# Linear attention and two MLPs on one core: the numerator in plain float32 on half arrays, and five k buffers

## The chip, the cores and the metric

The kernel runs on one core of a Trainium2 chip. The metric is the device time of one execution in microseconds, as the median of several runs. For the kernel before it is 980.39 us (3 runs, 980.27 to 983.37). Engines are named as in the profile: PE (TensorE; PEld are its weight loads), DVE (VectorE), ACT (ScalarE), POOL (GpSimd), SP (SyncE, which issues all transfers here).

## The reference

```python
def phi(x):                                   # 128 random features of each head
    h = einsum('bhsd,md->bhsm', x, omega) - sum(x * x) / 2
    return exp(h - max(h)) / sqrt(m)
q_p, k_p = phi(q * scale), phi(k * scale)     # 4 batches, 8 heads, 576 tokens, width 64
kv  = einsum('bhsm,bhsd->bhmd', k_p, v)
num = einsum('bhsm,bhmd->bhsd', q_p, kv)
den = einsum('bhsm,bhm->bhs', q_p, sum(k_p, axis=2)) + 1e-6
x = (num / den) as 2304 tokens x 512
x = mish(x @ w_in)  @ w_out                   # 512 -> 2048 -> 512
x = silu(x @ w2_in) @ w2_out                  # 512 -> 2048 -> 512
```

## The kernel before

The attention runs unit by unit. There are 36 k units (four batches of nine, each 128 tokens of four heads; the middle unit of a batch has 64 tokens for either group of heads). Each loads a buffer `kin`, projects it (`kproj`: two plain float32 products into `kpj`), takes the maximum and the bias on DVE, exponentiates on ACT into `kf`, and accumulates `kv` and the column sums (`kacc`, into `acc`). `k_finish` then copies the sum of a batch into `kv`, in a high part (`kvh`, ACT) and a low part (`kvl`, DVE), and spreads the denominators (`zb`, `zt`, `zz`). There are 36 q units: nine blocks of 256 tokens, two groups of four heads, two halves of 128 tokens. Each loads `qin`, projects (`qproj`: either plain float32, or split into high and low parts and three fast products), takes maximum, exponent and denominator, scales the features (`fn`), and transposes them on PE (`tr`, into `tp`); ACT copies the transposed features out (`hiT`). After the second half of a group the numerator (`num`, into `xp`) multiplies them with `kv`, and the result goes to a tile `X` in high and low parts (`xev`, `xlo`). Four steps of the first MLP (`H` and `Y`, products into `h` and `y`) follow for every block, with weights that were converted and split beforehand (`conv`, from `wr` to `wt` to `W`). When the attention is done, the rest of both MLPs runs in blocks of 512 columns.

The numerator exists in two forms. For the first two blocks (`NUM4 = 2`) it is four plain float32 products of 256 columns with a stationary operand of 128 columns (`num4`, tiles `FTf` and `kvf`): 64 columns of one head beside 64 columns of zeros, and the two heads of a pair add up into one 128-row result. For the other seven blocks it is split (`num`): high and low parts of the features (`hiT`, `loT`) and of `kv`, three fast products (`mm3`, the helper at lines 273 to 275, also used by the MLPs) for each head and pair, 12 in all, or 24 where a block crosses the border of two batches. Three of the nine blocks do. All features stand in one buffer `FT`, or one `FTf`.

The order of all instructions is written by a planner (`Plan`). Every task has an engine, a cost and a key (a due time; `KSPAN` is the span of a batch of k units in it, the table `OFF` adds to it, and `VAR` says which engine does a task). The planner simulates the engines, picks buffers from rings, and emits the tasks in the simulated order; on the chip each engine then runs its own list in order and waits for semaphores. `SHARED` is what it charges a DVE task that runs beside POOL. Where it foresees a gap on PE early on, it emits small filling products into a tile that is about to be written (line 420), which keep PE active and compute nothing. Transfers are all issued by SP in one list; one whose buffer is not free yet holds up those behind it. The `kin` ring has three buffers, and for the first seven units (`KIN0`) also the two `X` tiles.

Of the kernel before, what the change touches and what calls it, by code (L numbers as in the profile page):

```python
# [9 lines left out]
F32 = mybir.dt.float32  # L10
F32R = mybir.dt.float32r
# [8 lines left out]
P = 128  # L20
# [15 lines left out]
KSPAN = 7.6  # L36
EPS = 0.1

NUM4 = 2
# [4 lines left out]
VAR = dict(sqk="DPPDDDDDDDDDDAPDDDDDDDPPDDDDDDPDPPPP",  # L44
           sqq="DPDDPPDDDPDDDPPDDPDPDPPDADDPDPPDDDAA",
           den="DDDDDDDDDPDDPDDDDDDDPPDPPPDPDDDDDPDD",
           fn="PPPPPPPDPDPPDPPAPPPPDPPPDPPPDPPPDPPP",
           gl="PDDPDPDPDPDPDDDDPPPPPDDDDDDDDDDDPDDD",
           qlo="PDDDDPPPDPDDPDDDPPPPPDPDDPPDPDDPPDDP",
           wl="DDPDPDDPDPPPDDPP",  # L50
           wsg="DDDDDDDDDDDDDDDDDDDDDDDDDDDDDDDDDDDDDDDDDDDDDDDDD",
           xlo="DDDDDPDDDDDDDDPPPP",
           spl="S4444SSSSSSSSSSSSSSS4SSS44SSSSSSSSSS")
HORIZON = 21.0
OFF = {'H': -0.73, 'K*': -3.2, 'K0': -0.01, 'K1': 0.11, 'K10': -0.4, 'K17': -0.19, 'K28': -0.47, 'K4': 0.02, 'K7': -0.74,
# [11 lines left out]
       22.43, 'xll': -31.58, 'xlo': -8.73, 'xst': -1.34, 'xsth': -13.01, 'xstl': 8.31, 'xt': -2.1, 'zb': -3.35, 'zt': -1.62,  # L67
       'zz': 0.64}
# [4 lines left out]
SHARED = dict(wb0=0.8, wo0=0.6, ws0=0.5, wl0=0.5, wb1=0.8, wo1=0.6, ws1=0.5, gl=0.6, ksqr=2.5, qsqr=2.5, den=1.3, fn=0.6,  # L73
              qlo=0.5, xtbx=1.2, sa=1.5, kba=5.0, kbb=5.0, qba=5.0, qbb=5.0, dea=5.0)


def kind_of(name):
# [6 lines left out]
    if (k[0] == "q" and k not in ("qp", "qd")) or k in ("fz", "den", "dea", "der", "fn", "tr", "hiT", "loT", "num", "xev", "xlo", "xf", "xst"):  # L84
        return k, "Q*", "Q" + re.findall(r"\d+", name)[0]
# [178 lines left out]
def performer_two_mlps(ctx: ExitStack, tc: tile.TileContext, qin, kin, omT, w1, w2, out):  # L264
# [136 lines left out]
    D = 2.0  # L401
# [26 lines left out]
    T("FTf", "-", 0, -99, lambda: None, new=[("FTf", "FTf")], writes=["FTf"])  # L428
    T("FT", "-", 0, -99, lambda: None, new=[("FT", "FT")], writes=["FT"])
# [50 lines left out]
    def k_unit(b, j):  # L480
# [3 lines left out]
        if j == 0:  # L484
            def zero():
                POOL.memset(t[f"kv{b}"][:, :, :, 64:128].bitcast(F32), 0.0)

            T(f"kvo{b}", "Pool", 0.5, key, zero, writes=[f"kv{b}:{x}{g}" for x in "hl" for g in range(2)],
              new=[(f"kv{b}", "kv"), (f"z{b}", "z")])
            if not b:  # L490
                T("kvof", "Pool", 0.3, key, lambda: POOL.memset(t["kvf"][:, :, 64:128], 0.0), writes=["kvf:0", "kvf:1"], new=[("kvf", "kvf")])
# [36 lines left out]
    def k_finish(b, g, key):  # L528
# [8 lines left out]
        def kvh():  # L537
            src, dh, dl = parts()
            ACT.copy(dh, src)

        def kvl():
            src, dh, dl = parts()
            DVE.tensor_tensor(dl, src, dh.bitcast(F32), ALU.subtract)
# [593 lines left out]
```

## Time and profile before

| | kernel before |
|---|---|
| median of the runs | 980.39 us |
| the profiled execution, its own time | 987.46 us |
| its span, first to last instruction | 985.7 us |
| PE busy | 957.7 us (97%) |
| PEld / DVE / ACT / POOL busy | 890.0 / 631.5 / 519.2 / 327.8 us |
| granted clock, mean | 0.987 of full |
| moved by DMA | 102.56 MB, mean 104 GB/s |

Busy times of PE are to be read with care: the end of a product is modelled and lies behind the start of the next one, and filling products count as busy. What a product costs in a stream is the distance from its start to that of the next. Plain float32 products stand as two records each. The share of the whole span hides the stages: in the first 140 us the k units, the q units, the conversion of the weights and the loads are all under way together; after that PE is nearly without a gap.

### The profile page before, as it was taken

What the parts mean: (1) busy time and instruction counts of PE and PEld (TensorE: products, weight loads), DVE (VectorE), ACT (ScalarE), POOL (GpSimd) and SP (SyncE); (2) the same over time, 40 slices, a digit from 0 to 9 for tenths busy, and PEclk for the clock granted to TensorE, in tenths of its full rate; (3) what the DMA queues carried; (4) which work ended last, traced back from release to release, by engine and by line L of the source; (5) the groups of instructions that cost most, each with busy time, mean ns of one, the idle gap of its engine ahead of it and who ended that gap; (6) DMA issues with size and microseconds to landing.
All of it is one profiled execution on the core that took longest, in us unless ns stands there. A gap on an engine that the chain in (4) does not pass through costs nothing.

```text
span 985.7 us, 18121 instructions
## 1 busy us (share of the span) xinstructions
PE 957.7 (97%) x6671; PEld 890.0 (90%) x6671; DVE 631.5 (64%) x1686; ACT 519.2 (53%) x1128; POOL 327.8 (33%) x308
## 2 busy tenths in 40 slices
PE   7888999999999999999999989999999999999998
PEld 6777899999999999989899988898998898898898
DVE  6989876877776566744665789538446774353422
ACT  5676777787677655443444454445444543433221
POOL 2223213424553165430622374406223433213010
PEclk8999899999999999999999999999999999999999
DMA  7665335333231124205144244122332201311202
GB/s 248 209 221 186 103 110 165 97 109 110 94 118 55 44 87 126 99 22 192 44 150 150 87 134 131 57 86 65 108 108 86 86 22 44 125 58 54 86 1 86
DMA packets 50360, 102.56 MB, mean 104 GB/s; under 512 B 4960, under 2 KB 17504, under 8 KB 50272
## 3 DMA queue, kind: packets, MB, share of 16 engines
q1 hardware_dynamic: 50272, 101.41, 31.6%
q8 instruction: 52, 0.85, 0.4%
q14 instruction: 36, 0.29, 0.1%
HBM read 78.85 MB, written 22.54 MB: 103 GB/s over the span
## 4 chain that ended last, share of the span: by engine, by line
PE 78%; DVE 11%; DMA 4%; issue 3%; ACT 3%; POOL 1%; SPq 0%; POOLq 0%; DVEq 0%; ACTq 0%
PE y L275 12%; PE y L274 12%; PE y L273 12%; PE ha L273 5%; PE ha L274 4%; PE ha L275 4%; PE h L273 3%; PE h L274 3%; PE h L275 3%; PE hb L273 3%; PE hb L274 3%; PE hb L275 3%; DMA kin<-in_kin_dram 2%; PE acc L516 2%; PE kpj L505 2%
## 5 line engine op out<-in xcount | busy, mean ns | idle before, releaser
L843 DVE TENSOR_TENSOR gl<-e,gh 128x512 fp32r<-128x512 f32 x132 | 109.6, 837 | 142.3 <-ACT gh L841 140.3
L841 ACT CAST gh<-e 128x512 fp32r<-128x512 f32 x144 | 89.1, 623 | 177.8 <-PE y L274 171.3
L273 PE MATMUL y<-gh,W 128*128 128x256 f32 (+1 forms) x548 | 179.0, 327 | 0.0
L275 PE MATMUL y<-gl,W 128*128 128x256 f32 (+1 forms) x548 | 178.0, 325 | 0.0
L274 PE MATMUL y<-gh,W 128*128 128x256 f32 (+1 forms) x548 | 178.0, 325 | 0.0
L275 PEld LDWEIGHTS y<-gl,W 128*128 128x128 f32 x548 | 103.3, 189 | 9.6 <-DVE gl L843 0.2
L273 PEld LDWEIGHTS y<-gh,W 128*128 128x128 f32 x548 | 103.4, 189 | 8.3
L274 PEld LDWEIGHTS y<-gh,W 128*128 128x128 f32 x548 | 103.4, 189 | 8.2
L273 PE MATMUL h<-X,W 128*128 128x256 f32 x288 | 83.6, 290 | 0.0
L274 PE MATMUL h<-X,W 128*128 128x256 f32 x288 | 81.6, 283 | 0.0
L275 PE MATMUL h<-X,W 128*128 128x256 f32 x288 | 81.5, 283 | 0.0
L763 POOL TENSOR_TENSOR LHL<-Lqf,LX 128x512 fp32r<-128x512 f32 x19 | 25.4, 1343 | 161.4 <-ACT LX L762 161.1
L895 DVE TENSOR_TENSOR Lfz<-Lfz,ha 128x256 f32<-128x256 f32 x48 | 20.2, 420 | 84.2 <-PE ha L275 60.7
L736 ACT ACTIVATE wa<-wr 128x512 f32<-128x512 f32 x64 | 43.4, 681 | 51.9 <-DVE wt L747 29.6
L840 ACT ACTIVATE e<-hb 128x512 f32<-128x512 f32 x48 | 28.7, 598 | 51.8 <-DVE hb L895 51.8
L747 DVE SCALAR_TENSOR_TENSOR wt<-wa,wt 128x512 int32<-128x512 int32 x64 | 54.8, 861 | 0.9
L274 PEld LDWEIGHTS h<-X,W 128*128 128x128 f32 x288 | 55.0, 191 | 0.1
L273 PEld LDWEIGHTS h<-X,W 128*128 128x128 f32 x288 | 54.9, 191 | 0.1
L275 PEld LDWEIGHTS h<-X,W 128*128 128x128 f32 x288 | 54.9, 191 | 0.0
L505 PE MATMUL kpj<-cst,kin 128*128 128x256 f32 x144 | 41.4, 414 | 9.2 <-DMA kin<-in_kin_dram 8.0
L516 PEld LDWEIGHTS acc<-kin,kf 128*128 128x128 f32 (+1 forms) x320 | 42.1, 204 | 7.3 <-ACT kf L476 5.3
L648 POOL TENSOR_TENSOR qf<-qf,smq 128x512 f32<-128x512 f32 x28 | 31.2, 1117 | 50.9 <-DVE smq L639 13.9
(546 smaller groups left out, 3024.5 us busy)
## 6 DMA issues: line engine op xcount, KB each, us to landing
wr<-in_w_dram SPq DMA_DIRECT2D x64, 512.0 KB, 3.9
kin<-in_kin_dram SPq DMA_DIRECT2D x35, 386.0 KB, 3.9
qin<-in_qin_dram SPq DMA_DIRECT2D x36, 256.0 KB, 3.3
xf<-sx SPq DMA_DIRECT2D x18, 256.0 KB, 2.5
yp<-stg SPq DMA_DIRECT2D x18, 256.0 KB, 2.1
stg<-yp SPq DMA_DIRECT2D x18, 256.0 KB, 5.2
y<-stg SPq DMA_DIRECT2D x18, 256.0 KB, 2.4
Lqf<-y SPq DMA_DIRECT2D x17, 256.0 KB, 3.0
```

The costliest lines, as they stand in the source:

```text
L273: PE.matmul(o, s_hi, m_hi, start=first, stop=False, skip_group_check=True)
L274: PE.matmul(o, s_lo, m_hi, start=False, stop=False, skip_group_check=True)
L275: PE.matmul(o, s_hi, m_lo, start=False, stop=last, skip_group_check=True)
L505: PE.matmul(t[pj][:, jj * 256:(jj + 1) * 256], t[res][:, jj * P:(jj + 1) * P], t["cst"][:, P:P + 256], start=True, stop=True, skip_group_c ...
L516: PE.matmul(a[:, h, :], t[f][r0:r1, h * NF:(h + 1) * NF], v[r0:r1, h, :], start=first and h == 0, stop=last, skip_group_check=True)
L648: (DVE if fn_e == "DVE" else POOL).tensor_tensor(x, x, smq[:, r, 5, :, None].to_broadcast([P, 4, NF]), ALU.mult)
L736: T("wm" + c, "ACT", 0.57, key, lambda: ACT.activation(t[wa], t[raw][:, :, 1].bitcast(F32), AF.Copy, scale=2.0 ** -112), reads=[raw], writ ...
L747: T("ws" + c, "DVE", 0.6, key, lambda: DVE.scalar_tensor_tensor(t[wt], t[wa].bitcast(I32), 3, t[wt], ALU.logical_shift_left, ALU.bitwise_o ...
L763: T(f"sl{nm}", "Pool", 0.13 + 1.18 * n / DM, key, lambda: POOL.tensor_tensor(lo(), src(), hi().bitcast(F32), ALU.subtract), reads=res + [r ...
L840: T(f"X{s}.{x}", "ACT", 0.49, ks, lambda: ACT.activation(t[e], t[h], AFN), reads=res, writes=[e], new=[(e, "e")], tab=tab)
L841: T(f"gh{s}.{x}", "ACT", 0.52, ks, lambda: ACT.copy(t[gh[x]], t[e]), reads=[e], writes=[gh[x]], new=[(gh[x], "ghi")])
L843: T(f"gl{s}.{x}", dict(D="DVE", P="Pool")[low], dict(D=0.605, P=1.25)[low], ks, lambda: dict(D=DVE, P=POOL)[low].tensor_tensor(t[gl[x]], t ...
```

## The change

- The split numerator goes. All nine blocks use plain float32, and no zeros are multiplied: each head has its own product with a stationary operand of 64 columns, which writes rows 0 to 63 or 64 to 127 of the result. There are four such products of 256 columns for a numerator, or eight shorter ones at a border of batches.
- With it go `loT` (28 on DVE), `kvl` (8 on DVE), the second copy of the first batch `kvf` (2 on ACT) and the zeroing on POOL (5). `kv` and `FT` hold one part instead of two; `FT` has two buffers.
- The memory gained goes into the rings: `kin` has five buffers (seven at first, with the `X` tiles), `kf` four, `kv` and `z` four.
- The planner's costs change: the numerator at 1.2 us for every block, longer transfers, other charges for DVE beside POOL. `KSPAN` goes from 7.6 to 6.0, and `OFF`, `VAR`, the keys of later weights (`W1`, `W2`, `W3`) and the lead of the later inputs (`XLEAD`) are new. 14 instead of 7 q units are projected in plain float32 (`spl`).

```diff
-KSPAN = 7.6
+KSPAN = 6.0
-NUM4 = 2
+NUMC = 1.2
...
-           spl="S4444SSSSSSSSSSSSSSS4SSS44SSSSSSSSSS")
+           spl="S4444S4SS4S4SSSSSSSS4SSS4SSSS4S4444S")
...
-       'U': 8.86, 'W1.0': 0.51, 'W1.1': -0.05, 'W2.0': -0.15, 'W3.0': 0.93, 'W5.1': -0.56, 'W7.0': -0.05, 'W7.1': -0.05,
+       0.2, 'Q31': -2.92, 'Q32': 0.2, 'Q33': 0.2, 'Q34': 0.2, 'Q35': 0.2, 'Q7': 0.11, 'Q8': 0.11, 'U': 7.78, 'W1.0': 0.65,
...
-    ring("kin", tags("kin", 3), [P, KIN], F32)
-    ring("kin0", tags("kin", 3) + tags("X", 2), [P, KIN], F32)
-    ring("kf", tags("kf", 3), S2, F32)
+    ring("kin", tags("kin", 5), [P, KIN], F32)
+    ring("kin0", tags("kin", 5) + tags("X", 2), [P, KIN], F32)
+    ring("kf", tags("kf", 4), S2, F32)
-    ring("kv", tags("kv", 3), [P, 2, 4, 192], F32R)
-    ring("z", tags("z", 3), [P, 8, NF], F32)
+    ring("kv", tags("kv", 4), [P, 4, 2 * HD], F32)
+    ring("z", tags("z", 4), [P, 8, NF], F32)
-    ring("FT", ["FT"], [P, 2, 4, 256], F32R)
-    ring("FTf", ["FTf"], [P, 4, 256], F32)
-    ring("kvf", ["kvf"], [P, 4, 192], F32)
+    ring("FT", tags("FT", 2), [P, 4, 256], F32)
...
-            T(f"kld{n}", "DMA", 0.98, key - 3, lambda: nc.sync.dma_start(out=t[res], in_=kin[b, j]),
+            T(f"kld{n}", "DMA", 1.1, key - 3, lambda: nc.sync.dma_start(out=t[res], in_=kin[b, j]),
...
-        def kvl():
-            src, dh, dl = parts()
-            DVE.tensor_tensor(dl, src, dh.bitcast(F32), ALU.subtract)
+        def kvc():
+            ACT.copy(t[f"kv{b}"][:, 2 * g:2 * g + 2, :].rearrange("p c (a d) -> p c a d", d=HD),
+                     t[a][:, 0:4 * (HD + 1)].rearrange("p (c a d) -> p c a d", a=2, d=HD + 1)[:, :, :, 0:HD])
...
-            T(f"loT{n}", "DVE", 0.6, key, lambda: DVE.tensor_tensor(ft(1), src(), ft(0).bitcast(F32), ALU.subtract),
-              reads=[tp, f"FT:{i}h"], writes=[f"FT:{i}l"])
...
-                    for a in range(2):
-                        mm3(x[:, jj, t0:t1], kv[:, 0, c, 64 * a:64 * a + 128], kv[:, 1, c, 64 * a:64 * a + 128],
-                            th[:, 2 * jj + a, t0:t1], tl[:, 2 * jj + a, t0:t1], a == 0, a == 1)
...
+                        PE.matmul(x[HD * a:HD * a + HD, jj, t0:t1], t[f"kv{b}"][:, c, HD * a:HD * a + HD], t[FT][:, 2 * jj + a, t0:t1],
+                                  start=True, stop=True, skip_group_check=True)
...
-XLEAD = 12.1
+XLEAD = 5.2
```

The first place where the order moves is PE around the second numerator, the last of the first block, which the first product of the MLP (`h`) waits for. The program of before reads there (`kpj` is a k projection, `acc` an accumulation, `qpj` a q projection, `tp` a transpose, `xp` the numerator, rows with `om` alone are fillers):

```order
L420 MATMUL kpj_880<-om 128x256 x3
L505 MATMUL kpj_880<-cst,kin_837 128x256 x2
L420 MATMUL acc_1_755<-om 128x248 x3
L516 MATMUL acc_1_755<-kin_778,kf_886 128x65 x4
L505 MATMUL kpj_913<-cst,kin_860 128x256 x2
L655 MATMUL tp_929<-cst,qf_827 128x128 x4
L516 MATMUL acc_1_755<-kin_837,kf_924 128x65 x4
L697 MATMUL xp_945<-FTf,kvf 128x256 x4
L551 MATMUL zt_1_974<-cst,zb_1_950 128x128 x4
L505 MATMUL kpj_987<-cst,kin_918 128x256 x2
L516 MATMUL acc_0_997<-kin_860,kf_966 128x65 x4
L273 MATMUL h_1011<-X_813,W_87 128x256
```

The changed program reads at the same place:

```order
L536 MATMUL zt_1_829<-cst,zb_1_794 128x128 x4
L511 MATMUL acc_0_837<-kin_701,kf_811 128x65 x4
L500 MATMUL kpj_853<-cst,kin_765 128x256 x2
L511 MATMUL acc_0_837<-kin_714,kf_824 128x65 x4
L500 MATMUL kpj_882<-cst,kin_786 128x256 x2
L500 MATMUL kpj_887<-cst,kin_820 128x256 x2
L633 MATMUL tp_896<-cst,qf_770 128x128 x4
L422 MATMUL xp_907<-om 128x256 x5
L657 MATMUL xp_907<-FT_803,kv_109 64x256 x4
L422 MATMUL acc_0_837<-om 128x248 x4
L511 MATMUL acc_0_837<-kin_765,kf_922 128x65 x4
L500 MATMUL kpj_950<-cst,kin_865 128x256 x2
```

Ahead of the second numerator there now stand 23 k projections and 88 products of accumulations (22 groups of four) instead of 19 and 80, four `zt` groups instead of three, and one split q projection instead of two. Of the 73 fillers ahead of it five are left; four more follow later. Further down 16 numerators remain in both programs. DVE's list has 242 instructions ahead of the low half of that numerator's result (`xlo`), before it had 244: 24 instead of 19 k maxima, 46 instead of 38 small bias steps, five instead of six q maxima, 12 instead of 20 squares of q, 21 instead of 24 and 10 instead of 11 steps of weight conversion, and no low part of `kv` instead of three.

The second place is SP's list from its eighth row on, early in the program (`kin` are k loads, `wr` weight loads of the first MLP, `qin` q loads). Before:

```order
L734 DMA wr_0_1_159<-in_w_dram 128x1024
L499 DMA kin_173<-in_kin_dram 128x772
L734 DMA wr_1_0_176<-in_w_dram 128x1024
L734 DMA wr_1_1_186<-in_w_dram 128x1024
L499 DMA kin_233<-in_kin_dram 128x772
L734 DMA wr_2_0_251<-in_w_dram 128x1024
L499 DMA kin_272<-in_kin_dram 128x772
L499 DMA kin_287<-in_kin_dram 128x772
L734 DMA wr_2_1_298<-in_w_dram 128x1024
L581 DMA qin_319<-in_qin_dram 128x512
```

Changed:

```order
L494 DMA kin_154<-in_kin_dram 128x772
L688 DMA wr_0_1_164<-in_w_dram 128x1024
L494 DMA kin_175<-in_kin_dram 128x772
L494 DMA kin_182<-in_kin_dram 128x772
L688 DMA wr_1_0_190<-in_w_dram 128x1024
L688 DMA wr_1_1_214<-in_w_dram 128x1024
L559 DMA qin_228<-in_qin_dram 128x512
L559 DMA qin_244<-in_qin_dram 128x512
L494 DMA kin_258<-in_kin_dram 128x772
L494 DMA kin_285<-in_kin_dram 128x772
```

The k loads stand further ahead of the weight loads: seven k units are loaded ahead of the third weight load (`wr_1_0`), where it was five before.

## Rows read from the trace of the kernel before

**Rows 1.** Stages: us; busy time of PE, PEld, DVE, ACT, POOL; clock; DMA share; GB/s.

```profile
0.00:20.00 20.00, 14.46 (x62) 12.39 (x63) 12.47 (x55) 9.10 (x26) 3.57 (x12) 0.83 0.76 255
20.00:80.00 60.00, 50.56 (x326) 44.08 (x325) 54.23 (x263) 39.53 (x122) 16.68 (x17) 0.97 0.65 208
80.00:140.00 60.00, 57.47 (x388) 53.65 (x389) 51.16 (x246) 41.76 (x104) 16.63 (x17) 0.91 0.46 146
140.00:360.00 220.00, 216.44 (x1801) 213.20 (x1800) 154.11 (x531) 160.96 (x364) 84.21 (x85) 1.00 0.29 94
360.00:985.00 625.00, 618.75 (x4101) 566.62 (x4099) 359.48 (x595) 267.84 (x517) 206.72 (x179) 1.00 0.27 89
```

**Rows 2.** Who waits, 0 to 140 us: waiter, releaser: us, times, longest.

```profile
SPq L499 <- PE acc L516: 41.8, 20, 6.0
PE kpj L505 <- DMA kin<-in_kin_dram: 8.0, 5, 3.5
```

**Rows 3.** Chain that ended last, 0 to 145 us: start, us, what.

```profile
20.15 5.60 DMA kin<-in_kin_dram
...
45.00 6.66 DMA kin<-in_kin_dram
...
79.99 3.68 PE xp L697 x8
83.67 0.44 PE zt L551 x4
84.10 0.87 PE kpj L505 x4
...
128.66 1.73 PE xp L697 x8
130.39 0.85 PE acc L516 x8
```

**Rows 4.** Fillers on PE, instruction groups by form, 0 to 330 us.

```profile
L420 PE MATMUL acc<-om 128*128 128x248 f32 x32 | 6.3, 340 | 0.0
...
L420 PE MATMUL kpj<-om 128*128 128x256 f32 x34 | 5.2, 296 | 1.4 <-ACT qf L476 1.4
...
L420 PE MATMUL qpj<-om 128*128 128x256 f32 x7 | 1.2, 309 | 0.0
```

**Rows 5.** PE in order of time, split numerator at a border, its first and last.

```profile
145.99 0.28 PE L273 MATMUL xp<-FT,kv 128*128 128x64 f32 x1
...
148.62 0.27 PE L275 MATMUL xp<-FT,kv 128*128 128x192 f32 x1
148.73 0.47 PE L516 MATMUL acc<-kin,kf 128*128 128x65 f32 x3
```

**Rows 6.** PE in order of time, split numerator within one batch, 12 products.

```profile
172.44 0.28 PE L273 MATMUL xp<-FT,kv 128*128 128x256 f32 x1
...
173.73 0.28 PE L275 MATMUL xp<-FT,kv 128*128 128x256 f32 x1
173.85 0.60 PE L551 MATMUL zt<-cst,zb 128*128 128x128 f32 x4
```

**Rows 7.** PE in order of time: accumulations of 64 rows, on half arrays.

```profile
21.82 1.60 PE L516 MATMUL acc<-kin,kf 64*128 64x65 f32 x16
23.36 1.13 PE L505 MATMUL kpj<-cst,kin 128*128 128x256 f32 x4
...
59.02 1.10 PE L516 MATMUL acc<-kin,kf 64*128 64x65 f32 x8
60.05 1.13 PE L505 MATMUL kpj<-cst,kin 128*128 128x256 f32 x4
```

**Rows 8.** DVE, the low parts of the features, instruction groups, all time.

```profile
L669 DVE TENSOR_TENSOR FT<-tp,FT 128x512 fp32r<-128x512 f32 x28 | 19.0, 686 | 15.6 <-ACT FT L668 15.5
```

**Rows 9.** Granted clock around a gap: columns as in rows 1.

```profile
107.40:110.80 3.40, 2.56 (x23) 2.21 (x21) 3.40 (x18) 3.10 (x10) 0.77 (x1) 1.00 0.00 0
110.80:117.60 6.80, 6.80 (x28) 6.44 (x29) 4.38 (x16) 4.45 (x10) 1.89 (x2) 0.50 0.61 197
```

**Rows 10.** PE in order of time at the lower clock: a k unit's products.

```profile
110.75 2.08 PE L505 MATMUL kpj<-cst,kin 128*128 128x256 f32 x4 [0.32 <-ACT kf L476]
112.61 1.81 PE L516 MATMUL acc<-kin,kf 128*128 128x65 f32 x8
```

More of the change, by code (lines that the diff above doesn't have):

```diff
@@ L484, in k_unit @@
         if j == 0:
[L485 to L491, printed above, removed]
+            T(f"kvo{b}", "-", 0, 0, lambda: None, writes=[f"kv{b}:{g}" for g in range(2)], new=[(f"kv{b}", "kv"), (f"z{b}", "z")],
+              after=[f"kvo{b - 1}"] if b else [])
         kring = "kin0" if n < KIN0 else "kin"
@@ L529, in k_finish @@
         a, zb, zt = f"acc{b}.{g}", f"zb{b}.{g}", f"zt{b}.{g}"
-        def parts():
-            kv = t[f"kv{b}"]
-            src = t[a][:, 0:4 * (HD + 1)].rearrange("p (c a d) -> p c a d", a=2, d=HD + 1)[:, :, :, 0:HD]
-            dh, dl = [kv[:, x, 2 * g:2 * g + 2, :].rearrange("p c (a d) -> p c a d", d=64)[:, :, 0:3:2, :] for x in range(2)]
-            return src, dh, dl
-        def kvh():
-            src, dh, dl = parts()
-            ACT.copy(dh, src)
-        def kvl():
-            src, dh, dl = parts()
-            DVE.tensor_tensor(dl, src, dh.bitcast(F32), ALU.subtract)
+        def kvc():
+            ACT.copy(t[f"kv{b}"][:, 2 * g:2 * g + 2, :].rearrange("p c (a d) -> p c a d", d=HD),
+                     t[a][:, 0:4 * (HD + 1)].rearrange("p (c a d) -> p c a d", a=2, d=HD + 1)[:, :, :, 0:HD])
         def zbc():
@@ L551, in ztr @@
                 PE.transpose(t[zt][:, h * NF:(h + 1) * NF], t[zb][:, h * NF:(h + 1) * NF], t["cst"][:, 0:P])
-        T(f"kvh{b}.{g}", "ACT", 0.26, key, kvh, reads=[a], writes=[f"kv{b}:h{g}"])
-        if not b:
-            def kvf():
-                src = t[a][:, 0:4 * (HD + 1)].rearrange("p (c a d) -> p c a d", a=2, d=HD + 1)[:, :, :, 0:HD]
-                ACT.copy(t["kvf"][:, 2 * g:2 * g + 2, :].rearrange("p c (a d) -> p c a d", d=64)[:, :, 0:3:2, :], src)
-            T(f"kvf{g}", "ACT", 0.26, key, kvf, reads=[a], writes=[f"kvf:{g}"])
-        T(f"kvl{b}.{g}", "DVE", 0.35, key, kvl, reads=[a, f"kv{b}:h{g}"], writes=[f"kv{b}:l{g}"])
+        T(f"kvh{b}.{g}", "ACT", 0.26, key, kvc, reads=[a], writes=[f"kv{b}:{g}"])
         T(f"zb{b}.{g}", "ACT", 0.48, key, zbc, reads=[a], writes=[zb], new=[(zb, "zb")])
@@ L658, in q_unit @@
           fill=fill_of(lambda: t[tp][:, 0:256]))
-        def ft(x):
-            return t["FT"][:, x, :, i * P:(i + 1) * P]
-        src = lambda: t[tp].rearrange("p (h m) -> p h m", m=NF)
-        plain = blk < NUM4
-        if plain:
-            T(f"hiT{n}", "ACT", 0.48, key, lambda: ACT.copy(t["FTf"][:, :, i * P:(i + 1) * P], src()), reads=[tp, "FTf"], writes=[f"FTf:{i}"])
-        else:
-            T(f"hiT{n}", "ACT", 0.48, key, lambda: ACT.copy(ft(0), src()), reads=[tp, "FT"], writes=[f"FT:{i}h"])
-            T(f"loT{n}", "DVE", 0.6, key, lambda: DVE.tensor_tensor(ft(1), src(), ft(0).bitcast(F32), ALU.subtract),
-              reads=[tp, f"FT:{i}h"], writes=[f"FT:{i}l"])
+        FT = f"FT{n // 2}"
+        T(f"hiT{n}", "ACT", 0.48, key, lambda: ACT.copy(t[FT][:, :, i * P:(i + 1) * P], t[tp].rearrange("p (h m) -> p h m", m=NF)),
+          reads=[tp], writes=[f"{FT}:{i}"], new=[] if i else [(FT, "FT")])
         if not i:
@@ L686, in num @@
                 for b, t0, t1 in cols:
[L687 removed]
                     for a in range(2):
[L689 to L707 removed]
+                        PE.matmul(x[HD * a:HD * a + HD, jj, t0:t1], t[f"kv{b}"][:, c, HD * a:HD * a + HD], t[FT][:, 2 * jj + a, t0:t1],
+                                  start=True, stop=True, skip_group_check=True)
+        T(f"num{n}", "PE", NUMC, key, num, reads=[f"{FT}:0", f"{FT}:1"] + [f"kv{b}:{g}" for b, _, _ in cols],
+          writes=[xp], new=[(xp, "pt0" if n < QEARLY else "pt")], fill=fill_of(lambda: t[xp][:, 0:256]))
         def xs(x):
@@ L974, in evac @@
             src, res = dram_ap(yp_d if ph == 1 else yq_d, "dy" if ph == 1 else "dq", st, i, epb)
-            T("ld" + g, "DMA", 0.67, key - 3, lambda: nc.sync.dma_start(out=v(), in_=src), reads=res, writes=[g], new=[(g, "stg")],
+            T("ld" + g, "DMA", 0.73, key - 3, lambda: nc.sync.dma_start(out=v(), in_=src), reads=res, writes=[g], new=[(g, "stg")],
               after=[f"Ma{s}.0"], lat=D)
@@ L985, in evac @@
             dst, res = dram_ap(yp_d if ph == 0 else yq_d, "dy" if ph == 0 else "dq", st, i, epb)
-        T("st" + g, "DMA", 0.67 * m / DM, key, lambda: nc.sync.dma_start(out=dst, in_=v()), reads=[g], writes=res, lat=D)
+        T("st" + g, "DMA", 0.73 * m / DM, key, lambda: nc.sync.dma_start(out=dst, in_=v()), reads=[g], writes=res, lat=D)
     xlast = []
@@ L1003, in fetch @@
                 src, res = y1_d[bi][:, 2 * (a - 1):2 * a, 256 * b:256 * b + 256], [f"dz{bi}:{c}.{b}" for c in (2 * a - 2, 2 * a - 1)]
-            T("xl" + x, "DMA", 0.67, ks, lambda: nc.sync.dma_start(out=t3(x).bitcast(F32), in_=src), reads=res, writes=[x],
+            T("xl" + x, "DMA", 0.73, ks, lambda: nc.sync.dma_start(out=t3(x).bitcast(F32), in_=src), reads=res, writes=[x],
               new=[(x, "xs")], lat=D, after=["att"] + prev)
```

69 lines of the change are left out of this document (25 added, 44 removed), and 16 rows, old and new, of the table OFF.

## The prediction

> **What bounds the kernel now.** I read the stages first [rows 1]. From 140 us on PE is busy 216.4 of 220 us and then 618.8 of 625 us: there the kernel is as long as its products. What is taken from PE's list in that stretch comes off the end, unless another engine takes over. The stage ahead of it is different. From 20 to 80 us DVE is busy 54.2 of 60 us and PE 50.6, and PE's figure flatters: it holds the 73 fillers of [rows 4], 12.7 us of busy time that computes nothing. So up to about 80 us PE waits for other engines, and from 80 to 140 us it turns into the bound (57.5 of 60 us, partly at a lower clock).
>
> Next, who holds up the first stage. SP stands 41.8 us in front of k loads whose buffer an accumulation still reads, and PE waits 8.0 us for `kin` [rows 2]. The chain has two k loads on it in the first 80 us, 5.60 and 6.66 us [rows 3]. Both point at the three `kin` buffers. But DVE has only 5.8 us idle from 20 to 80 us [rows 1], so faster loads alone cannot pull this stage in by much.
>
> The point that splits the two stages is the second numerator, the last of block 0, which PE starts at 79.99 us [rows 3]: what PE does ahead of it fits into gaps, what it does after it counts in full. I cost the change on either side of that point, against the span of 985.7 us; the profiled run lies 1.8 us above its span and 7.1 us above the median.
>
> **The numerator, after that point.** Sixteen of 18 are left. Before, two are plain: 8 records in 1.73 us [rows 3], which is 0.216 a record, 3.5 us in all. Eight lie within one batch: 172.44 to 173.85 is 1.41 us [rows 6], 11.3 us. Six cross a border: 145.99 to 148.73 is 2.74 us [rows 5], 16.4 us. Together 31.2 us.
>
> After, 256 columns on half the array are still 256 columns to stream, so a numerator has the same 8 records as the plain one and costs 1.73 us if nothing overlaps. Whether the two halves overlap is the largest unknown. The trace of before has no products on 64 columns, but it has some on 64 rows [rows 7]. A run of 8 records takes 1.03 us (59.02 to 60.05), where 8 on the whole array take 0.85 us [rows 3]: going onto halves and back costs 0.18 us. A run of 16, in which the second 8 use the other half, takes 1.54 us (21.82 to 23.36). Without overlap it would be 0.18 + 2 x 0.85 = 1.88 us, so 0.34 us ran side by side. Halves can overlap, and here the heads alternate between them.
>
> How far? One end is full overlap: 1.73 / 2 + 0.18 = 1.05 us. The other is none: 1.91 us. Between them, if records start strictly in turn (two of one half, two of the other), a second record runs beside the first of the next head, and 5 record times pass instead of 8: 1.08 + 0.18 = 1.26 us. I take this one, since the run of 16 overlapped only in part. For a border with 64 and 192 columns I take 0.106 us for a short record (0.85 / 8 [rows 3]) and 0.162 for three quarters of a long one: 16 records are 2.14 us, minus 0.85 for the seven overlaps is 1.29, plus 0.18 is 1.47. With 128 and 128 columns, at 0.11 us a record, 1.76 - 0.77 + 0.18 = 1.17. The sum is 10 x 1.26 + 4 x 1.47 + 2 x 1.17 = 20.8 us, a **saving of 10.4 us**. Full overlap gives 10.5 + 5.0 + 2.1 = 17.6 us and saves 13.6; none gives 19.1 + 9.3 + 3.9 = 32.3 and loses 1.1.
>
> The Trainium skill ("TensorE: Matmul & The Clock Gate", Part 3, The mechanism) says that matmuls start and end strictly in program order, which is the case in turn; its measured packing speeds (2.38 times for three column tiles) are for one product per tile. No run here shows columns; by free halves the forecast below would be 3.2 us lower.
>
> **Work moved ahead of that point.** By the two lists four k projections (0.87 us each), two accumulations (0.85) and one `zt` (0.44) more stand ahead of the second numerator [rows 3], and one split q projection fewer (6 x 0.118 = 0.7, by the pace of [rows 6]): 3.5 + 1.7 + 0.4 - 0.7 = **4.9 us off the part that counts**. It costs nothing where it goes: the fillers alone were 73 x 0.12 = 8.8 us of PE's time there, at the pace of [rows 6], and all but five are gone from it. What DVE must do for block 0 hardly changes: five more k maxima, one q maximum fewer, fewer squares of q and conversions. So DVE reaches the low half of block 0 no later.
>
> **Plain q projections.** Seven more are plain: 0.87 against 0.71 us, **1.1 us added**. They free a copy on ACT and a subtraction on DVE or POOL, beside PE's work: nothing.
>
> **The k buffers.** At most 5.60 + 6.66 = 12.3 us of the chain go [rows 3], and DVE's 5.8 us of idle from 20 to 80 us limits that. Below nothing: the k loads stand ahead of weight loads in SP's list, and if the first weights arrive later, `h` waits; 3 us later is my bound, about half of one of the two k loads. DVE has little to give, so I take **3 us earlier**, bounds 10 earlier and 3 later.
>
> **DVE, ACT and POOL.** The 28 subtractions `loT` (19.0 us [rows 8]) go from DVE, eight `kvl`, two copies and five memsets besides. From 140 to 360 us DVE is busy 154 of 220 us and PE idle 3.6 us [rows 1]. At most those 3.6 us return; I take 0.8. What becomes late next is PE itself.
>
> **The sum.** -10.4 - 4.9 + 1.1 - 3.0 - 0.8 = -18.0 us: a span of 967.7 us. Scaled to the median, 18.0 x 980.4 / 987.5 = 17.9, so **962.5 us**.
>
> **The rivals.**
>
> *The first stage gives back more.* The k loads leave the chain and the halves overlap fully: -13.6 - 4.9 + 1.1 - 10 - 0.8 = -28.2, 952 us. For it: the 41.8 us that SP waits. Against: DVE at 90% from 20 to 80 us.
>
> *The halves don't overlap.* Then the change doesn't do what it says: +1.1 - 4.9 + 1.1 - 3.0 - 0.8 = -6.5, 974 us, still faster through the moved work and the loads. Against it stands the run of 16 [rows 7].
>
> *Other engines take half of the gain.* The k units, now ahead, and the q units share DVE, ACT and POOL; if PE then waits for a block's features half of what it saved, 9 us remain: 971.5 us. Against: DVE is busy only 70% from 140 to 360 us.
>
> *Slower: PE runs at the lower clock until block 0 is done.* In [rows 9] PE worked 2.56 of 3.40 us, then the granted clock was 0.50 for 6.8 us, that is 1.2 GHz instead of 2.4. The fillers that kept PE active are nearly all gone, and without them its work from 20 to 80 us is some 38 us of 60. At the lower clock a k unit takes about 1.86 + 1.61 = 3.5 us of PE (112.61 - 110.75, and 1.81 less the 0.2 by which an end is modelled too late) [rows 10], against 1.72 at full clock. 23 units ahead of the second numerator are then 80 us; with the q units, transposes and sums about 95, from 10 us on. It starts at 105 instead of 80 us: +25 - 10.4 - 4.9 + 1.1 - 0.8 = +10, 990 us. It decides once the low clock holds for most of that stage; a few such stretches fall into PE's waiting and cost nothing. The Trainium skill ("TensorE: Matmul & The Clock Gate", Part 1) states the rule: half clock is the default, and activity releases it. In the trace PE kept a mean of 0.97 from 20 to 80 us [rows 1], with fillers.
>
> **How the numbers follow.** Forecast 0.57; more given back 0.15; no overlap 0.12; half lost to other engines 0.08; slower 0.08. A measurement of this kernel can tell about 0.3% from no change, so faster means under 977.4 us and slower over 983.3. The first two cases are faster in full, the third and fourth at 974 and 971.5 mostly: 0.57 + 0.15 + 0.09 + 0.06 = 0.87. Same gets 0.05, slower 0.08. The range leaves out the slower case and the worst of the third: 951 to 976 us.
>
> **What would show it.** Right, if the numerators of 256 columns stand about 1.26 us from their first record to the next product, the second numerator starts between 70 and 83 us, and the span falls by the sum of both sides. The halves are wrong if records of the two heads never start within a few ns of each other. The loads are wrong if SP still waits over 30 us in 140 us for accumulations. The clock rival is right if the granted clock from 20 to 80 us falls below 0.7. What breaks the forecast beyond these is a new wait in the later blocks, whose weights and inputs are also ordered anew: there every microsecond that PE waits counts in full.

## The result, and the profile after

| | before | after |
|---|---|---|
| median of the runs | 981.1 us (980.3 to 983.4) | 951.3 us (950.9 to 951.6) |
| the profiled execution, its own time | 987.5 us | 951.2 us |
| its span | 985.7 us | 949.4 us |
| granted clock, mean | 0.987 | 0.996 |

The ratio of the medians is 0.969 [0.967, 0.971]: 29.8 us faster, where 18 were forecast. By the two profiled executions it is 36.3 us. The profiled execution of before lay 6.3 us above its median and that of after on it, so some 6.5 of the 36.3 us are no gain. Most of that is clock: in the 82 executions of before that were timed beside the experiments, the mean granted clock goes from 0.979 to 0.998 (median 0.993), and the time falls by some 6 us for each 0.01 of it. At 0.987 the profiled execution ran longer at the lower clock than the usual one, by that slope worth some 4 us.

The stages of the kernel after, columns as in [rows 1]:

```profile
0.00:20.00 20.00, 14.72 (x75) 12.05 (x76) 12.86 (x72) 8.92 (x25) 2.70 (x9) 1.00 0.88 304
20.00:80.00 60.00, 51.26 (x337) 44.14 (x336) 59.14 (x281) 48.87 (x161) 17.70 (x19) 0.94 0.74 238
80.00:140.00 60.00, 58.28 (x449) 52.87 (x448) 51.28 (x251) 51.55 (x148) 14.38 (x14) 1.00 0.51 165
140.00:360.00 220.00, 218.25 (x1852) 209.65 (x1851) 147.37 (x444) 160.53 (x360) 102.51 (x96) 1.00 0.30 95
360.00:949.00 589.00, 583.55 (x3809) 529.49 (x3807) 333.31 (x564) 249.50 (x478) 187.95 (x160) 1.00 0.27 87
```

From 20 to 80 us DVE is now busy 59.1 of 60 us (54.2 before): the first stage is as long as DVE's work. PE has 51.3 busy us there with nine fillers in all, against 50.6 with 73. From 80 us on the clock is at its full level throughout.

The second numerator, and a later one at a border, with what follows each, in order of time on PE:

```profile
71.95 1.08 PE L657 MATMUL xp<-FT,kv 128*64 128x256 f32 x8 [0.82 <-ACT FT L639]
72.96 0.73 PE L422 MATMUL acc<-om 128*128 128x248 f32 x4
...
137.29 1.10 PE L657 MATMUL xp<-FT,kv 128*64 128x64 f32 x16
138.33 0.39 PE L275 MATMUL y<-gh,W 128*128 128x256 f32 x1
```

From start to start the first takes 1.01 us, the border 1.04 (1.02 to 1.04 for all six). In the single records the two heads' products start about 6 ns apart: the halves run side by side in full. All 18 numerators take 18.2 us, before 36.6.

What the two kernels did up to the second numerator, columns as in [rows 1], before:

```profile
0.00:79.99 79.99, 65.01 (x386) 56.47 (x386) 66.69 (x317) 48.62 (x146) 20.25 (x29) 0.94 0.68 220
```

and after:

```profile
0.00:71.95 71.95, 57.92 (x348) 49.01 (x348) 63.96 (x311) 52.19 (x168) 17.23 (x24) 0.95 0.80 263
```

DVE idled 13.3 us up to that point before, and 8.0 after; it also did 2.7 us less. The two add up to the 8.0 us by which the numerator starts earlier.

The waits of the first 140 us that answer to [rows 2]:

```profile
SPq L494 <- PE acc L511: 53.3, 24, 7.4
PE kpj L500 <- DMA kin<-in_kin_dram: 4.2, 3, 2.6
```

SP stands longer in front of k loads than before (53.3 against 41.8 us), since it asks for them earlier. PE waits less for their data.

**One account for all kernels.** The experiments below are read with five numbers, added up from PE's records: when the second numerator starts; how much work (without numerators) PE's list has ahead of it, at the full-clock pace of each kind of product; the time after it in which PE ran nothing (from the modelled end of one record to the next start); and the time after it at the lower clock. The last microsecond or so of the program, at the lower clock in some runs, is not counted. Start minus work ahead (what PE spent up to there on anything else), plus idle, plus half the low-clock time is what PE lost. What is left of the span is PE's own work. Each row is one profiled execution, the median beside it is of all.

| kernel | median | start | ahead | idle after | low after | lost | left of the span |
|---|---|---|---|---|---|---|---|
| before | 981.1 | 80.0 | 44.4 | 9.9 | 13.7 | 52.4 | 933.3 |
| after | 951.3 | 71.9 | 49.7 | 6.2 | 0 | 28.4 | 921.0 |
| whole arrays | 961.0 | 71.6 | 49.7 | 4.7 | 0 | 26.6 | 932.0 |
| numerator alone | 982.8 | 64.3 | 37.7 | 21.6 | 17.1 | 56.8 | 920.9 |
| old tables | 975.1 | 71.7 | 44.6 | 18.1 | 13.7 | 52.1 | 923.0 |
| old rings | 970.8 | 67.9 | 37.7 | 10.3 | 2.8 | 41.9 | 925.4 |
| old rings, horizon 20 | 989.4 | 73.8 | 39.3 | 20.0 | 24.3 | 66.7 | 923.4 |
| four k buffers | 968.0 | 68.4 | 46.3 | 16.2 | 6.8 | 41.7 | 923.9 |
| span 7.6 | 967.5 | 70.4 | 44.6 | 14.3 | 6.8 | 43.5 | 922.2 |
| numerator charged 1.02 | 964.2 | 73.0 | 48.8 | 11.1 | 6.8 | 38.7 | 924.7 |
| horizon 20 | 956.1 | 79.7 | 53.1 | 8.0 | 3.4 | 36.3 | 921.3 |

The last column is the test of the account: it stays between 919 and 926 us for every kernel with half arrays that was run, whatever its order, while their times go from 951 to 990. So by the account the half arrays took some 11 to 12 us off PE's own work, and all other differences are in what PE lost; why it was lost, the account does not say. The column is good to 2 or 3 us: between whole and half arrays PE's records differ by 13.3 us in the numerators (first experiment), the column differs by 11.0.

### The profile page after: what moved, and what is told of

It is laid out like the page before. It is cut to its first block, busy times and chain, and to the rows that moved or that the text cites. A ratio compares the mean times of both kernels' runs of the same rounds, so it can differ in the third digit from the quotient of the medians.

```text
span 949.4 us, 17714 instructions
## 1 busy us (share of the span) xinstructions
PE 926.1 (98%) x6513; PEld 848.2 (89%) x6513; DVE 604.0 (64%) x1606; ACT 519.4 (55%) x1167; POOL 325.2 (34%) x297
## 4 chain that ended last, share of the span: by engine, by line
PE 81%; DVE 9%; issue 2%; DMA 2%; POOL 2%; ACT 2%; SPq 1%; DVEq 0%; POOLq 0%; ACTq 0%
PE y L275 12%; PE y L276 12%; PE y L277 12%; PE ha L275 4%; PE ha L277 4%; PE ha L276 4%; PE h L275 4%; PE h L277 4%; PE h L276 4%; PE hb L275 3%; PE hb L277 3%; PE hb L276 3%; PE acc L511 2%; PE kpj L500 2%; PE xp L657 1%
## 5 line engine op out<-in xcount | busy, mean ns | idle before, releaser
L797 DVE TENSOR_TENSOR gl<-e,gh 128x512 fp32r<-128x512 f32 x132 | 105.6, 807 | 122.5 <-ACT gh L795 122.4
L275 PE MATMUL y<-gh,W 128*128 128x256 f32 (+1 forms) x528 | 171.4, 325 | 0.2 <-DVE stg L931 0.2
L276 PE MATMUL y<-gh,W 128*128 128x256 f32 (+1 forms) x528 | 169.6, 321 | 0.0
L277 PE MATMUL y<-gl,W 128*128 128x256 f32 (+1 forms) x528 | 169.6, 321 | 0.0
L275 PEld LDWEIGHTS y<-gh,W 128*128 128x128 f32 x528 | 99.2, 188 | 9.2 <-issue 1.0
L277 PEld LDWEIGHTS y<-gl,W 128*128 128x128 f32 x528 | 99.1, 188 | 8.8
L276 PEld LDWEIGHTS y<-gh,W 128*128 128x128 f32 x528 | 99.2, 188 | 7.6
L717 POOL TENSOR_TENSOR LHL<-Lqf,LX 128x512 fp32r<-128x512 f32 x14 | 18.3, 1311 | 141.9 <-ACT LX L716 141.3
L276 PEld LDWEIGHTS h<-X,W 128*128 128x128 f32 x288 | 54.2, 188 | 0.2
L693 DVE TENSOR_SCALAR wt<-wr 128x512 int32<-128x512 int32 x64 | 38.5, 609 | 20.7 <-POOL W L717 16.9
L701 DVE SCALAR_TENSOR_TENSOR wt<-wa,wt 128x512 int32<-128x512 int32 x64 | 50.7, 801 | 0.8
L626 POOL TENSOR_TENSOR qf<-qf,smq 128x512 f32<-128x512 f32 x25 | 27.2, 1093 | 53.1 <-DVE smq L617 17.6
```

The lines of the kernel that those rows point to most:

```text
L275: PE.matmul(o, s_hi, m_hi, start=first, stop=False, skip_group_check=True)
L276: PE.matmul(o, s_lo, m_hi, start=False, stop=False, skip_group_check=True)
L277: PE.matmul(o, s_hi, m_lo, start=False, stop=last, skip_group_check=True)
L626: (DVE if fn_e == "DVE" else POOL).tensor_tensor(x, x, smq[:, r, 5, :, None].to_broadcast([P, 4, NF]), ALU.mult)
L693: sign = dict(D=lambda: DVE.tensor_scalar(t[wt], t[raw][:, :, 1], -0x80000000, None, ALU.bitwise_and), A=lambda: ACT.activation(t[wt].bitc ...
L701: T("ws" + c, "DVE", 0.6, key, lambda: DVE.scalar_tensor_tensor(t[wt], t[wa].bitcast(I32), 3, t[wt], ALU.logical_shift_left, ALU.bitwise_o ...
```

## The experiments

Unless said otherwise each kernel is the changed one with the edit shown. The planner writes a new order whenever a number of its own changes.

**Half arrays against whole ones, order held.** Each product gets the stationary operand of both heads, so that it writes all 128 rows, and the second head overwrites the first; otherwise the lists are the same row for row.

```diff
-PE.matmul(x[HD * a:HD * a + HD, jj, t0:t1], t[f"kv{b}"][:, c, HD * a:HD * a + HD], t[FT][:, 2 * jj + a, t0:t1],
+PE.matmul(x[:, jj, t0:t1], t[f"kv{b}"][:, c, :], t[FT][:, 2 * jj + a, t0:t1],
```

> The changed kernel with the numerator's products on the whole array: the stationary operand is both heads' 128 columns and the second head's product overwrites the first head's rows, so the numerator's values are not the reference's; the number, the lengths and the order of all instructions stay. Theory (two column halves run side by side, and PE is the bound after the second numerator): a numerator of 256 columns goes from 1.01 to about 1.73 us, one at a border from 1.03 to 1.7 to 2.2 us; 16 of them after the second numerator are about 13 us, the time 964 us (961 to 967). Rival (the new order and the rings bring the gain, and the numerator lies beside other work): under 955 us.

961.0 us (960.5 to 962.5). A later numerator of this kernel:

```profile
121.08 1.95 PE L657 MATMUL xp<-FT,kv 128*128 128x256 f32 x8
122.86 1.03 PE L579 MATMUL qpj<-cst,qin 128*128 128x256 f32 x4
```

This one takes 1.78 us; those of 256 columns take 1.54 to 1.78. All 18 take 31.5 us, 13.3 more than on half arrays, and the time rises by 9.7. Three quarters of what PE does less in a numerator reach the end. The theory holds, at the low end of what it expected.

**One half first.** The loop over the heads goes outside, so that all products of one half stand ahead of those of the other.

```diff
-            for jj in range(2):
-                c = 2 * g + jj
-                for b, t0, t1 in cols:
-                    for a in range(2):
+            for a in range(2):
+                for jj in range(2):
+                    c = 2 * g + jj
+                    for b, t0, t1 in cols:
```

> The changed kernel with the same products in another order: all of the first head of each pair (rows 0 to 63), then all of the second (rows 64 to 127). If PE starts products strictly in the order of its list, only the hand-over overlaps: 8 records in about 1.6 us instead of 1.01, some 10 us more, 961 us. Rival: each half takes its own records as soon as it is free, looking ahead in the list: 1.0 us a numerator and 951 us.

953.9 us (0.970 [0.965, 0.974]). A numerator within one batch, and one at a border:

```profile
119.81 1.09 PE L657 MATMUL xp<-FT,kv 128*64 128x256 f32 x8
120.83 1.13 PE L579 MATMUL qpj<-cst,qin 128*128 128x256 f32 x4
...
136.99 1.60 PE L657 MATMUL xp<-FT,kv 128*64 128x64 f32 x16
138.52 0.39 PE L275 MATMUL y<-gh,W 128*128 128x256 f32 x1
```

It takes 2.6 us more than after. Eight records still take 1.02 us: the single records start in four pairs, 13 ns apart within a pair, one of either half, although four records of the first half stand ahead of the other's in the list. With 16 records it takes 1.53 us instead of 1.04, so the reach is limited: four records of the first half start alone, and the other half sets in beside the fifth. This was the forecast's "free halves" against its "in turn", and the free halves have it. The Trainium skill ("TensorE: Matmul & The Clock Gate", Part 3, The mechanism) says that matmuls start strictly in program order. The 1.02 us of this run do not agree, and the measurement decides: eight records in list order would take about 1.7 us (seven record times of 0.216 and the 0.18 for going onto halves and back).

**The numerator alone.** The old rings (three `kin`, three `kf`, the rest of the memory left unused until the attention is done) and the planner's old numbers; only the arithmetic of the numerator is new.

```diff
-    ring("kin", tags("kin", 5), [P, KIN], F32)
-    ring("kin0", tags("kin", 5) + tags("X", 2), [P, KIN], F32)
-    ring("kf", tags("kf", 4), S2, F32)
+    ring("kin", tags("kin", 3), [P, KIN], F32)
+    ring("kin0", tags("kin", 3) + tags("X", 2), [P, KIN], F32)
+    ring("kf", tags("kf", 3), S2, F32)
+    ring("pad", tags("pad", 3), S2, F32)
...
-KSPAN = 6.0
+KSPAN = 7.6
```

(`VAR`, `OFF`, `SHARED`, `W1` to `W3`, `XLEAD` and the costs of the transfers go back too; the rings of `kv`, `z` and `FT` and the numerator's charge stay new.)

> The changed kernel with both the old tables of the plan and the old number of k and feature buffers: the half-array numerator alone on the kernel before. Theory (the numerator takes some 17 us of PE's time after the second one, and that counts where PE has no other wait; with tables made for other costs new waits take part of it): 965 to 975 us. Rival (rings and tables are worth nothing without each other, the numerator brings its full saving): 962 to 965 us.

982.8 us, 0.999 [0.997, 1.002] of before: nothing at all, where both theories expected a gain. Yet its numerators are as short as those of after, and PE's own work is 12 us shorter in the account. Two later stretches, columns as in [rows 1], show places where that was lost:

```profile
200.00:220.00 20.00, 13.01 (x87) 9.96 (x83) 19.93 (x58) 14.52 (x45) 13.58 (x13) 0.83 0.34 98
220.00:240.00 20.00, 15.04 (x103) 14.42 (x103) 11.92 (x25) 9.45 (x19) 8.97 (x8) 0.83 0.13 40
```

and PE's longest waits there (waiter, releaser: us, times, longest):

```profile
PE h L272 <- ACT e L792: 6.0, 2, 4.8
PE tp L631 <- POOL qf L624: 3.0, 1, 3.0
PE tp L631 <- ACT qf L474: 2.2, 1, 2.2
```

From 200 to 220 us DVE is busy 19.93 of 20 us and PE only 13.0: a shorter list on PE runs into the other engines, here ACT and POOL, and the clock falls behind the gaps (0.83).

**Rings or tables alone.** First the old rings with the new numbers, then the new rings with the old numbers (the two halves of the edit above).

> The changed kernel with three k buffers (five at first) and three feature buffers as before; the tables of the plan are those of the change, and the planner orders anew for the smaller rings. Theory (the k buffers bring the second numerator and the k work ahead of it forward, 5 to 10 us): 956 to 962 us. Rival (the tables and the numerator bring all): within 3 us of 951.

> The changed kernel with the planner's tables of before (KSPAN 7.6, OFF, VAR, charges beside POOL, transfer costs, keys of later weights and inputs); half-array numerator and rings as in the change. Theory (the tables move k work ahead of the second numerator, some 5 us, and the rest comes from the numerator and the rings): 956 to 960 us. Rival (the tables bring most of the gain): over 965 us.

970.8 us (967.5 to 973.1) and 975.1 us (972.7 to 977.0), both above what was expected by theory. With three buffers the second numerator starts 4 us earlier than in after, but with 12 us less work ahead of it. With the old numbers PE idles 18.1 us later on and runs 13.7 us at the lower clock. Against the numerator alone (982.8) the rings bring 7.7 us, the numbers 12.0, and both together 31.5: each is worth more beside the other.

**The span of a batch alone.**

```diff
-KSPAN = 6.0
+KSPAN = 7.6
```

> The changed kernel with KSPAN 7.6 instead of 6.0 alone, so that k units come later. By the two lists 3.9 us less of PE's work then stands ahead of the second numerator. Theory (what is moved ahead counts in full): 955 to 957 us. Rival (the gain of the tables lies elsewhere): 951 to 953 us; if the low clock comes back after 80 us, over 958.

967.5 us: 16.2 more, against 4 to 6 expected. 5.1 us less of PE's work stand ahead of the second numerator, which starts 1.5 us earlier; later PE idles 8.1 us more and runs 6.8 us at the lower clock.

**The fillers.** `FILL_END` at -1.0 switches them off, once in the kernel after and once in that of before.

```diff
-FILL_END, FILL_MIN, FILL_PART, FILL_COST, FILL_MAX = 140.0, 0.35, 0.75, 0.12, 24
+FILL_END, FILL_MIN, FILL_PART, FILL_COST, FILL_MAX = -1.0, 0.35, 0.75, 0.12, 24
```

> The changed kernel without its nine filling products. Theory (they lie in a wait and the clock holds without them): 950 to 952 us. Rival (they keep the clock up for the second numerator and what follows): over 955 us, with a granted clock under 0.9 from 80 to 140 us.

> The kernel before without its 73 filling products. Theory (PE waits for DVE and the loads in the first 80 us, so a lower clock there costs little): within 5 us of the kernel before, with a granted clock of 0.6 to 0.8 from 20 to 80 us. Rival (the low clock makes PE the bound of the first stage): more than 10 us slower than before.

After without its nine: 952.7 us (951.7 to 955.2), just above the 950 to 952 of the theory; from 80 to 140 us the granted clock is 1.00, against the rival. Before without its 73: 983.0 us, 0.999 [0.996, 1.002]. Its stretch from 20 to 80 us:

```profile
20.00:80.00 60.00, 48.02 (x244) 40.17 (x242) 54.73 (x263) 41.98 (x125) 17.82 (x19) 0.80 0.69 228
```

The clock falls to 0.80 there, with 23.9 us at the lower level ahead of the second numerator, and that numerator starts at 76.9 us, no later than with fillers. The lower clock falls into PE's waiting and costs nothing that shows. The forecast's slower case needs a clock that stays low for most of the stage; even without fillers it did not. What such a clock would cost was not run.

**Does any new order cost as much?** The losses of 16 to 24 us so far might not belong to the buffers or the span: their numbers were found for one order, and every edit makes another. So two numbers with no resource behind them were changed, and two doses of the suspects run beside them.

```diff
-NUMC = 1.2
+NUMC = 1.02
```

> The changed kernel, but the planner is told that a numerator costs 1.02 us, as measured, and not 1.2 us. No buffer, due time or product changes; the planner still writes another order (over half of PE's list stands elsewhere). It asks whether the losses of 16 to 24 us of the earlier runs belong to the numbers that were put back there, or to any new order. By the theory that the k buffers and the due times themselves carry the gain, this one stays near 951.3 us: 948 to 956. By the rival, that every table was fitted to this one order and any other order pays for it, it goes to 960 to 972, as the runs with old buffers or the old span of a batch did.

```diff
-HORIZON = 21.0
+HORIZON = 20.0
```

> The changed kernel, but the planner looks 20 us ahead instead of 21 us (HORIZON). A second number with no resource behind it. By the theory of buffers and due times 949 to 957 us. By the rival, that any new order pays, 960 to 972.

```diff
-    ring("kin", tags("kin", 5), [P, KIN], F32)
-    ring("kin0", tags("kin", 5) + tags("X", 2), [P, KIN], F32)
+    ring("kin", tags("kin", 4), [P, KIN], F32)
+    ring("kin0", tags("kin", 4) + tags("X", 2), [P, KIN], F32)
+    ring("pad", tags("pad", 1), S2, F32)
```

> The changed kernel with four k buffers instead of five (six instead of seven with the X tiles); kf, kv and z keep four. Three k buffers and three kf gave 970.8 us, 19.5 us over the changed kernel. If the buffers carry that, one buffer fewer lies between: 955 to 964 us, and the second numerator has some 45 to 49 us of PE's work ahead of it (41.8 with three, 51.6 with five). If any new order costs as much, it lies where the two runs with a number changed lie.

```diff
-KSPAN = 6.0
+KSPAN = 6.4
```

> The changed kernel with the span of a batch of k units at 6.4 us instead of 6.0; 7.6 gave 967.5 us, 16.2 us over. This change of order is the smallest of all (292 of 5,779 rows of PE's list). If the span carries the 16.2 us in proportion, a quarter of it is 4 us: 953 to 957. If any new order pays, 960 to 972. If only the second numerator's place matters, under 953, since it hardly moves here.

964.2, 956.1, 968.0 and 958.0 us. The charge of 1.02 us is the measured cost of a numerator, and it is 12.9 us worse; the horizon costs 4.8 and the span of 6.4 us 6.7. So a new order by itself costs 5 to 13 us, and the single runs above prove less about buffers and span than they seemed to. My theory had allowed 5 us.

**The same perturbations with three buffers, and with the old span.** If buffers carry time of their own, orders that nobody fitted must differ as well.

> The changed kernel with the old rings (three k buffers, three kf) and HORIZON 20. With five buffers the same HORIZON gave 956.1 us. If the buffers carry time of their own, this one lies as far above it as three buffers lay above five in the fitted order, 12 to 20 us: 968 to 976. If the loss with three buffers was the price of an order that the tables were not fitted to, both unfitted orders lie together: 953 to 964.

> The changed kernel with the old rings and a numerator charged 1.02 us. With five buffers that charge gave 964.2 us. Buffers of their own: 972 to 984. Price of an unfitted order: 955 to 970.

> The changed kernel with the old rings and a span of 6.4 us. With five buffers that span gave 958.0 us. Buffers of their own: 968 to 976. Price of an unfitted order: 954 to 965.

> The changed kernel with five k buffers, the old span of 7.6 us and HORIZON 20. If the span carries time of its own, 966 to 974; if 967.5 us with this span alone was the price of an unfitted order, near the three unfitted ones at 6.0 and 6.4 us (956.1, 958.0, 964.2): 953 to 965.

> The changed kernel with five k buffers, the old span of 7.6 us and a numerator charged 1.02 us. With a span of 6.0 us that charge gave 964.2 us. If the span carries time of its own, 970 to 986; if not, 955 to 966.

> The changed kernel with four k buffers and HORIZON 20. Five gave 956.1 us with it, three (with three kf) 989.4 us. If each buffer carries a part, 966 to 980; if the fifth carries nothing and the step is from three to four, 953 to 962.

| numbers of the planner | five `kin` | four | three (and three `kf`) | five, span 7.6 |
|---|---|---|---|---|
| as in the change | 951.3 | 968.0 | 970.8 | 967.5 |
| HORIZON 20 | 956.1 | 968.3 | 989.4 | 977.6 |
| NUMC 1.02 | 964.2 | | 980.0 | 979.4 |
| KSPAN 6.4 | 958.0 | | 989.7 | |

In every row three buffers are slower than five, by 19.5, 33.3, 15.8 and 31.7 us, 25 in the mean; four lie between in both rows with them. The old span is slower in all three rows, by 16.2, 21.5 and 15.2. These are larger than the 5 to 13 us of an unfitted order, so beside the new numbers both carry time of their own; three of the six runs came out above even the range that I gave for that case (989.4, 989.7 and 977.6). With three buffers and new numbers the mean is 982.5 us, no better than before: what the half arrays save is lost again there.

A fifth pair stands among the runs above, and it speaks less clearly. With the old numbers, which come from the kernel with three buffers, three give 982.8 and five 975.1 us: 7.7 us, no more than a new order can cost, and start minus work ahead is 26.6 and 27.1 us, the same. So what the buffers are worth depends on the numbers beside them. The half arrays with three buffers and numbers fitted to both were not run, so part of the 16 to 33 us may be the fit to five buffers.

Three buffers against five under HORIZON 20, from 20 to 80 and from 140 to 360 us, columns as in [rows 1]. Three:

```profile
20.00:80.00 60.00, 52.55 (x299) 44.45 (x298) 52.61 (x241) 40.53 (x132) 17.92 (x18) 0.83 0.63 200
...
140.00:360.00 220.00, 206.86 (x1642) 192.51 (x1643) 130.01 (x500) 150.70 (x363) 78.45 (x75) 0.96 0.28 92
```

Five:

```profile
20.00:80.00 60.00, 57.07 (x394) 51.39 (x395) 58.64 (x279) 47.12 (x156) 18.11 (x19) 0.97 0.77 240
...
140.00:360.00 220.00, 216.25 (x1825) 205.97 (x1824) 152.97 (x475) 161.46 (x375) 100.70 (x96) 1.00 0.32 101
```

With three, DVE is busy 52.6 instead of 58.6 us in the first stage; from 140 to 360 us DVE and PE are behind as well (130.0 against 153.0, 206.9 against 216.3 us). Two stretches of that time with three buffers:

```profile
200.00:220.00 20.00, 14.17 (x87) 10.98 (x86) 17.46 (x72) 15.92 (x46) 8.09 (x9) 0.83 0.32 104
...
300.00:320.00 20.00, 15.62 (x98) 11.46 (x97) 8.45 (x49) 13.97 (x34) 1.04 (x1) 0.83 0.15 53
```

In the first PE is busy 14.2 of 20 us beside a DVE at 17.5, and the clock drops after the gaps; the second shows that later gaps occur with no engine full, so a single busy engine is not the whole story. Why three buffers lead to these gaps so much later is not shown.

## Why the prediction was right and wrong

The direction and the two sides of the second numerator held. The sum was too small on both sides: it took the halves to overlap only in part, and it priced the first stage and the waits and the clock after it at a fraction of what they gave.

- **The numerator after that point** was taken at -10.4 us; the 16 later ones fell from 31.5 to 16.2, **-15.3**. The step that failed is the choice between the bounds: "I take this one, since the run of 16 overlapped only in part". One numerator of 256 columns takes 1.01 us, just under the 1.05 of full overlap; PE looks past records of the busy half, which the run with one half first shows. That -15.3 is more than even the best bound, -13.6, because borders cost some 1.03 us, where full overlap was priced at 1.25 (2.14 / 2 + 0.18) and 1.06: a short record of 64 columns was priced at 0.106 us from products with 128 stationary columns, but on a half the next one starts 0.055 us later (on the whole array 0.111). Shorter weight loads (136 against 190 ns below) would explain that; it was not tested by itself.
- **Work moved ahead of it**, 4.9 us by the two lists: 5.3 by the account (49.7 against 44.4). Right, and so was the point that it fits there: the start did not move back.
- **The plain q projections**, +1.1 us: not measured apart.
- **The k buffers**, -3.0 us: the numerator starts **8.0 us** earlier, inside the bounds. "DVE has little to give" failed: DVE gave 5.3 us of idle time, nearly all of it from 20 us on, and had 2.7 us less to do, which I had set at nothing. The larger mistake is that I priced the buffers only up to that point. Beside the new numbers the pairs of orders put them (with the fourth `kf`) at 16 to 33 us over the whole run, beside the old ones at 7.7. Of the 16 to 33, 8 to 11 us are there by the second numerator (start minus work ahead, 34.5 against 26.6 under HORIZON 20), the rest in idle time and low clock after it, for which I had no term.
- **DVE, ACT and POOL**, -0.8 us: idle time after the second numerator fell by 3.7 us, and the time at the lower clock from 13.7 us to none, worth 6.9. The clock's part, [rows 9], had no term in the sum at all; some 4 us of it belong to the profiled execution of before and not to the change (see the result). How much of it is due to the fitted order stays open: three unfitted orders with five buffers have 3.4 to 6.8 us of low clock and 1.8 to 4.9 us more idle time.
- **The scaling.** 18.0 us of span became 17.9 of the median. In fact the profiled execution of before was slower than its median by more than such terms are worth, and 36.3 us of span are 29.8 of the median.

By the account of the two profiles the 36.3 us are 12.3 of PE's own work, 13.4 up to the second numerator (8.0 earlier, 5.3 more work done by then), 3.7 of idle time and 6.9 of clock. Of the rivals, the first stage giving back more (952 us) came about in size, with its reason, the loads, and full overlap as well, though part of it lies behind the first stage. That its 952 us lie so close is partly luck: its sum of 28.2 us holds nothing for the 10.6 us of idle time and clock, and the median shows 29.8 of the profile's 36.3 us. Halves without overlap is refuted by the first run, which prices it: 961 us, not 974. Other engines taking half came about where I did not look for it: with three buffers and the old numbers, waits and clock take all of the gain (982.8 us, no change from 982.6 of before, timed beside it). The slower case did not come about: from 20 to 80 us the clock was 0.94, without fillers 0.94 too, and 0.80 in the kernel before without fillers.

Of the signs that I named, the start (70 to 83 us) and the clock (0.94 from 20 to 80 us) read as I said. The numerator of 256 columns did not (1.01 us, not 1.26), nor the wait of SP: it rose to 53.3 us, and by my rule the loads would be wrong. A queue that asks earlier waits longer; PE's wait for `kin`, which halved, was the one to name. No k load of 5 us or more is left on the chain between 20 and 75 us.

What stays open: how the 30 us divide between numerator, buffers and numbers. They do not add up: without buffers and numbers the numerator brings 0, with whole arrays the rest brings 21 (961.0 against 981.9, timed beside it), and without the rings or without the numbers 11 and 7 are left (970.8 and 975.1). No version that was run beats the changed kernel; the order that its numbers give beats the three neighbours that were run by 4.8 us or more.

## What to carry to other kernels

A shorter list on the bound engine is worth what the others can follow: price a saving together with the buffers that let them, and look for the wait that takes its place later in the run. Where a planner writes the order, undoing one number measures a new order too; run the same meaningless change with and without the part in question before a difference of 5 to 13 us is put down to it. And a profiled execution 0.6% above its median makes terms of a few microseconds uncertain by as much; its granted clock beside that of the other executions tells whether the clock is the reason.

## What was not expected of the hardware

- Plain float32 products on the two column halves of the array run fully side by side, also where four records of one half stand ahead of the other's in the list (1.02 us for eight), but only in part where eight do (1.53 against 1.04 us for 16).
- A weight load of 64 columns takes 136 ns in the kernel after, one of 128 columns in the kernel with whole arrays 190 ns (instruction groups by form: busy us, mean ns of one | idle us before it; of after from 140 to 360 us, then of whole arrays from 80 to 360 us):

```profile
L657 PEld LDWEIGHTS xp<-FT,kv 128*64 128x64 f32 x144 | 8.2, 136 | 3.1
```

```profile
L657 PEld LDWEIGHTS xp<-FT,kv 128*128 128x128 f32 x176 | 27.3, 190 | 1.7
```

- 23.9 us at the lower clock ahead of the second numerator cost the kernel before without fillers nothing that shows (983.0 against 982.6 us): its second numerator starts no later. In the account 2.8 to 24.3 us of it after that point go with slower times.
